# The last iterations of the front, and a new order of the block sums, in a fused attention, mixture-of-experts and softplus kernel

## The chip, the cores and the metric

The kernel runs on one core of a Trainium2 chip. The metric is the time of one execution on the device in microseconds (us); of several executions the median counts. A profile is one further execution, recorded by the hardware profiler. PE is TensorE, PEld its weight loads, DVE VectorE, ACT ScalarE, POOL GpSimd and SP SyncE.

## The reference

Three layers follow each other, in float32.

```
attention:  k, v averaged over blocks of 8 positions (576 -> 72); softmax(q k'/8) v'
            4 batches, 8 heads, 576 positions, 64 channels -> x of 2304 tokens x 512
mixture:    P = exp(x w_gate - max); 8 times: rows /= sum, columns /= sum, P *= 2304/8
            out = sum over 8 experts e of P[:, e] * (relu(x w1[e]) w2[e])     w1 512x1024, w2 1024x512
softplus:   out = softplus(x w_in) w_out                                      512x2048, 2048x512
```

## The kernel before

**Products.** A matrix product in float32 precision is three matmuls on parts: each operand is a rounded high part (`hi`, type fp32r) and a remainder (`lo`), and `three` adds hi*hi, lo*hi and hi*lo in PSUM (names such as `xhi`, `w1lo`, `hhi`, `hlo`). ScalarE rounds, GpSimd or VectorE subtracts for the remainder. All these matmuls stand at line L797.

**Block sums.** The first product of a layer is done with seven products of blocks in place of eight (Strassen's scheme). The input, cut into 2x2 blocks, gives the sums t1 to t4 (`t1 = b12 - b11`, `t3 = b22 - b12`, `t2 = b22 - t1`, `t4 = b21 - t2`), the weights of a unit give S1 to S4, and the products A11, A12, A22, S1, S2, S3, S4 (six matmuls of 128x384 each) are put together by VectorE: `u1 = pb + a` after S1, then after S3 `a = pb + a` (`za` in the rows), `pb = pc + a` and `pd = pd + a` (two rows `p<-p,za`), and at last S4 is added onto `pc` and `u1` onto that.

**Phases.** Work goes in units of 256 columns of the hidden layer, for three groups of 768 tokens: the mixture for group 0, then groups 1 and 2, then softplus for the three. In the two phases of groups 1 and 2 of the mixture (`TWICE`, about 620 to 1560 us) the second product has the block scheme too: two units form a pair, an even and an odd one, and a pair has seven "forms" (`h_slot`, numbered 0 to 6) which are made from the units' results by VectorE, rounded by ScalarE, and multiplied by forms of w2 (`form_product`, twelve matmuls).

**The order of the work** is written out by hand; each engine runs its instructions in program order. The loop `todo` issues `first n+1` before `second n`. `first_twice` issues the products of a unit; `second_twice` of an even unit issues forms 0 and 1, of an odd one forms 2 to 6, and after the first form product of each it calls `go_on`, which issues S4 of the unit whose `first_twice` went before. Between the products lie `posts`: `odd_posts` and `even_posts` multiply the results of a unit by the shares of its expert (`shared`, tile `pb`, L889) and make forms. What `odd_posts` leaves over goes into the list `later`, which the next even unit's `first_twice` works off: `s2` (form 5, ScalarE and GpSimd), `s4` (VectorE difference `d1 - s3`, rounding of form 6), `s1` (VectorE sum into `a21`, named `a` in the rows, form 4) and the remainder of form 6 (VectorE, L896). The shares of an expert, 128 copies of 768 numbers, are loaded by `load_shares` from the last odd unit of the expert before.

**The front** is the start: attention of steps m = 0 to 11 (`front(k)`: scores and softmax of step k, transposes of k - 2, the mixing product `px` of k - 2), whose results are tokens 0 to 767 of x, the input of group 0. In its last iterations (11 to 13, `AHEAD` is 12) it also does the beginning of unit 0 through `fill`. The other attention steps follow inside the first phase: `hook()` runs the next quarter of a step, or an entry of the list `side` (the gate's normalisation: `sk_max`, `sk_max_t`, ...).

Of the kernel before, what the change touches and what calls it, by code (L numbers as in the profile page):

```python
# [19 lines left out]
def attention_moe_softplus_kernel(  # L20
# [223 lines left out]
        pool_sub(lo, raw_form(q), hi.bitcast(F32))  # L244
        load_form(q + 4)

    def load_shares(i):
        if i < len(TWICE) * E:
            m, e = divmod(i, E)
            n = LARGE // P  # L250
            src = pd.rearrange("(t e) p -> e t p", e=E)[e, m * n:(m + 1) * n]
            nc.sync.dma_start(
                pb[0].rearrange("p (t n) -> p t n", n=P), src.partition_broadcast(P)
            )

    def load_w(which, n):
# [249 lines left out]
    def turn_attn():  # L506
# [6 lines left out]
            nc.scalar.copy(aT[:, h, :], pa[:SP, :W])  # L513
        to_mix.append((m, aT))

    def mix():
        m, aT = to_mix.pop(0)
        hb, hp = divmod(m, HP)
        vp = vp_t[kv_of(m)]
        px = bank("px")  # L520
        for h in range(2):
            nc.tensor.matmul(px[h * D:(h + 1) * D, :W], vp[:, h, :], aT[:, h, :])  # L522

        t0 = hb * W
        here = max(0, min(W, TP0 - t0))
        x0 = x_of(0)
        if here < W and hp == 0:
            xb[hb] = at_p.tile([P, KC, W], F32, tag="xb", name="xb")
        if here:
            nc.scalar.activation(x0[:, hp, t0:t0 + here], px[:, :here], AF.Copy, scale=1.0 / POOL)  # L530
        if here < W:
            nc.scalar.activation(xb[hb][:, hp, :], px[:, :W], AF.Copy, scale=1.0 / POOL)
        if here:
            tb = TP0 // 2
            for j in range(2):
                a, z = max(t0, j * tb), min(t0 + here, (j + 1) * tb)
                if a < z and (hp // 2, j) in first_x:
                    hi, lo = (t[:, hp % 2, a - j * tb:z - j * tb] for t in first_x[hp // 2, j])
                    src = px[:, a - t0:z - t0]
                    nc.scalar.activation(hi, src, AF.Copy, scale=1.0 / POOL)  # L540
                    nc.vector.scalar_tensor_tensor(
                        lo, src, 1.0 / POOL, hi.bitcast(F32), op0=ALU.mult, op1=ALU.subtract
                    )
        if hp == HP - 1:
            if here < W:
                nc.sync.dma_start(xd[:, :, max(0, t0 - TP0):t0 + W - TP0], xb[hb][:, :, here:])
            to_gate.append((t0, x0[:, :, t0:t0 + W] if here == W else xb[hb]))
# [25 lines left out]
    def attention():  # L573

        for m in range(AHEAD, STEPS + 2):
            now = [i for i in pooled_at if pooled_at[i] == m]
            while to_gate:
                gate()
            if m + 1 < STEPS:
                channels_first(m + 1)  # L580
            if m < STEPS:
                softmax(m)
            yield
            while to_exp:
                to_exp.pop(0)()
            while to_turn:
                turn_attn()
            for i in pooled_at:
                if pooled_at[i] == m - 1:
                    keys_turned(i)  # L590
            for i in now:
                keys_reduced(i, 0)
            yield
            while to_divide:
                to_divide.pop(0)()
            for i in now:
                values(i)
            yield
            while to_mix:
                mix()  # L600
            for i in now:
                keys_reduced(i, 1)
            yield
# [8 lines left out]
    def front(k, fill=(None, None)):  # L612

        if k < AHEAD:
            softmax(k)
        if to_turn:
            turn_attn()
        if fill[0]:
            fill[0]()
        if k + 1 <= AHEAD:  # L620
            channels_first(k + 1)
        while to_exp:
            to_exp.pop(0)()
        for i in keys_at.get(k, ()):
            keys_summed(i)
        warm((3, 3, 2, 1)[k] if k < 4 else 0)
        while to_divide and (len(to_divide) > 1 or k >= AHEAD):
            to_divide.pop(0)()
        while to_gate:
            gate()  # L630
        if to_mix:
            mix()
        if fill[1]:
            fill[1]()
# [213 lines left out]
    def first_twice(n, between):  # L848

        product = product_of(n)  # L850
        a, u1 = (zpool.tile([P, TB], F32, tag="z", name=x) for x in ("za", "u1"))
        kind = "RL"[sets[n][3] // 2 % 2]
        d1 = two_banks(kind, "p")
        pa, pd_ = d1[:, 0], d1[:, 1]
        product(pa, A11, "b11")
        between(0)
        product(pd_, A22, "t4")
        nc.scalar.copy(a, pa)
        between(1)
        for _ in range(2):  # L860
            if later:
                later.pop(0)()
        d2 = two_banks(kind, "p")
        pc, pb = d2[:, 0], d2[:, 1]
        product(pb, S2, "t2")
        between(2)
        product(pc, S1, "t1")
        vadd(u1, pb, a)
        run_later()
        between(3)  # L870
        product(pa, A12, "b21", True)
        between(4)
        product(pb, S3, "t3", True)
        vadd(a, pb, a)
        vadd(pb, pc, a)
        vadd(pd_, pd_, a)
        between(5)
        two_t[n] = d1, d2

        def s4():  # L880
            product(pc, S4, "b22", True)
            vadd(pc, pc, u1)

        return s4
# [35 lines left out]
    def odd_posts(n):  # L920
# [2 lines left out]
        q = pair_of_units(n) * FORMS  # L923
        d1, d2 = two_t.pop(n)

        def p1():
            shared(d1, d1, 0)
            form_hi(q + 2, d1)

        def p2():  # L930
            shared(d2, d2, 1)
            form_hi(q + 3, d2)
            if u % UPE == UPE - 1:
                load_shares(TWICE.index(f) * E + u // UPE + 1)

        def p3():
            form_lo(q + 2, d1, nc.vector)
# [13 lines left out]
            vsub(d1, d1, s3_t())  # L951
            form_hi(q + 6, d1)

        later.extend([s2, s4, s1, lambda: form_lo(q + 6, d1, nc.vector)])
        return [p1, p2, p3]

    def m_at(f, k):
# [71 lines left out]
                    prep_w2(n + 1)  # L1029
                    load_w(2, n + 2)  # L1030

    def first_parts(n):

        product = product_of(n)
        at = h_tiles(n)
# [21 lines left out]

        def a22():
            product(ps("d"), A22, "t4")

        def s3():
            product(ps("b"), S3, "t3", True)
            add(a, ps("b"), a)
            add(ps("b"), ps("c"), a)
            add(ps("d"), ps("d"), a)

        def a12():
# [22 lines left out]
    def first(n, between, done=None):  # L1090

        do = done or first_parts(n)
        order = ("s2", "a22", "s3") if done else ("m1", "s2", "s1", "a22", "s3", "a12")
        for k, x in enumerate(order):
            do[x]()
            between(k)
# [222 lines left out]
    def finish_attention():  # L1319
# [2 lines left out]
        for i in (2, 3):  # L1322
            g_t[i] = gp.tile([P, GW], F32, name=f"g{i}")
        pools.append(ctx.enter_context(tc.tile_pool(name="tmp", bufs=2)))
        side.extend([to_tiles] + [None] * 6 + [to_prob, None, sk_max, None, sk_max_t, None, None, sk_max_b, None])
        for _ in range(ITERS):
            side.extend([sk_rows, None, None, None, sk_cols])
        side.append(shares_out)
# [68 lines left out]
    def t_lo(eng, name, i, c):  # L1397
# [14 lines left out]
    loads = {  # L1412
# [4 lines left out]
    }  # L1417

    def load(what, i):
# [4 lines left out]
        else:  # L1424
            load_kv(i, k_t if what == "k" else v_t)

    for it in range(AHEAD + 2):
        fill = (None, None)
        if it == AHEAD - 1:
            def fill_in():  # L1430
                xs.update(xs_next)
                unit0.update(first_parts(0))
                unit0["m1"]()
                t_hi("t1", 0, 0)
                t_lo(nc.gpsimd, "t1", 0, 0)
            fill = (fill_in, None)
        if it == AHEAD:
            def fill_in():
# [5 lines left out]
        if it == AHEAD + 1:  # L1444
            def fill_in():
# [1 line left out]
                unit0["s1"]()  # L1447
                t_hi("t2", 1, 0)
                t_lo(nc.vector, "t2", 1, 0)
                t_hi("t4", 3, 0)  # L1450
                t_lo(nc.vector, "t4", 3, 0)
                t_hi("t3", 2, 0)
                t_lo(nc.gpsimd, "t3", 2, 0)
            fill = (fill_in, None)
        front(it, fill)
        if it in (0, 1, 2, 3):
# [10 lines left out]
        for what, i in loads.get(it, ()):  # L1467
            load(what, i)
        if it == 9:
            ectx.close()  # L1470
            hpool = ctx.enter_context(tc.tile_pool(name="h", bufs=1, side="right"))
            zpool = ctx.enter_context(tc.tile_pool(name="z", bufs=2, side="right"))
# [3 lines left out]
            ta, tb = (fpool.tile([P, 2, 2, TP0 // 2], F32, name=x) for x in ("ta", "tb"))  # L1476
            t0_of = lambda i: (ta, tb)[i // 2][:, i % 2]
        if it == 10:
            sums_w1(1)
            parts[1] = w1_parts(1)  # L1480
            x0_sum[1](0)
        if it == 11:
            x0_sum[1](1)
        if it in (12, 13):
            c = it - 12
            x0_sum[2](c)
            x0_sum[4](c)
            x0_sum[3](c)
    t_hi("t2", 1, 1)
    t_lo(nc.vector, "t2", 1, 1)  # L1490
    t_hi("t4", 3, 1)
    t_lo(nc.vector, "t4", 3, 1)
    hook()
    t_hi("t3", 2, 1)
    t_lo(nc.gpsimd, "t3", 2, 1)
    fctx.close()
    h2pool = ctx.enter_context(tc.tile_pool(name="h2", bufs=1, side="right"))
    h_at.append([h2pool.tile([P, UC, LARGE], F32R, name=f"h{x}1") for x in ("hi", "lo")])
# [64 lines left out]
    for step, (what, n) in enumerate(todo):  # L1563
# [3 lines left out]
        if what == "first":  # L1567
# [55 lines left out]
            def between(k):  # L1623
# [2 lines left out]
                    to_split.pop(0)()  # L1626
                if kind == "sp":
                    hook()
                if n or k > 1:
                    hook()  # L1630

            rest = first(n, between, None if n else unit0)
# [14 lines left out]
        else:  # L1647
# [46 lines left out]
                pending.pop(0)()  # L1694
            ahead(f, kind, u)
            if f == 0 and u == NU1 - 6:
                load_shares(0)
            if f == 0 and u == NU1 - 6:
                f64_t.pop()
            if twice(n + 1):  # L1700
# [37 lines left out]
```

## Time and profile before

| | before |
|---|---|
| median of 3 runs | 1955.19 us (1953.75 to 1955.24) |
| profiled execution | 1954.04 us |
| its span, first to last instruction | 1952.3 us |
| TensorE busy | 1928.6 us, 99% |
| weight loads busy | 1794.4 us, 92% |
| VectorE busy | 1471.4 us, 75% |
| ScalarE busy | 973.6 us, 50% |
| GpSimd busy | 1475.1 us, 76% |
| DMA | 306.56 MB, mean 157 GB/s |
| front, with unit 0 | about the first 65 us |
| pairs of units | one every 29.5 us, 32 pairs |

Busy time counts an instruction's whole record. Matmuls are pipelined and their records overlap, so a busy TensorE need not be at its peak; the distance from the start of one matmul to the next tells more. The time outside the span (1.7 us) belongs to the start and the end of the execution.

### The profile page before, as it was taken

To read this page: it belongs to the slowest core of one execution; us is meant where nothing else is said; L and a number is where in the kernel's file an instruction comes from. 1 tells how busy PE (TensorE), PEld (TensorE's weight loads), DVE (VectorE), ACT (ScalarE), POOL (GpSimd) and SP (SyncE) were. 2 spreads that over 40 slices of the span, in tenths; PEclk is the share of its full clock that TensorE was granted. 3 is DMA by queue.
4 is the path that set the end of the run, shared out by engine and by line. 5 is a ranking of instruction groups with operands and counts; after the bars stand their busy time and mean duration, and the time that the engine had idled before them with its cause. 6 is when DMAs were issued, how large, how long until landed. Compare 5 with 4: busy or idle time off the path is not lost.

```text
span 1952.3 us, 30469 instructions
## 1 busy us (share of the span) xinstructions
PE 1928.6 (99%) x10954; PEld 1794.4 (92%) x10954; DVE 1471.4 (75%) x2339; ACT 973.6 (50%) x1773; POOL 1475.1 (76%) x1142
## 2 busy tenths in 40 slices
PE   9899999999999999999999999999999999999999
PEld 7687888989989999999999999999999999999997
DVE  7775576887667888878988889888789776556455
ACT  6545435433334545545445655455554565565542
POOL 6776667787877788778787798887787879675563
PEclk9999999999999999999999999999999999999999
DMA  7343434555547655554555655555545523523311
GB/s 205 116 150 125 145 125 136 178 178 173 183 151 260 208 165 166 168 181 150 163 176 160 219 168 167 161 174 165 181 153 163 192 93 122 191 89 119 133 65 65
DMA packets 213347, 306.56 MB, mean 157 GB/s; under 512 B 33308, under 2 KB 147532, under 8 KB 212940
## 3 DMA queue, kind: packets, MB, share of 16 engines
q1 hardware_dynamic: 203116, 290.85, 46.4%
q10 hardware_dynamic: 10080, 13.77, 1.9%
q8 instruction: 86, 1.41, 0.3%
q14 instruction: 65, 0.53, 0.1%
HBM read 239.30 MB, written 65.27 MB: 156 GB/s over the span
## 4 chain that ended last, share of the span: by engine, by line
PE 90%; DVE 3%; POOL 2%; ACT 2%; DMA 1%; issue 1%; SPq 0%; ACTq 0%; DVEq 0%; POOLq 0%
PE py L797 45%; PE p L797 42%; POOL w1lo L289 1%; PE px L522 1%; PE s L477 1%; DMA vt<-in_v_dram 1%; PE pa L512 1%; DMA pb<-pd 0%; DVE p L1045 0%; POOL w2lo L289 0%; ACT w1hi L320 0%; DMA w2raw<-td 0%; PE pq L464 0%; ACT xhi L693 0%; DVE za L1045 0%
## 5 line engine op out<-in xcount | busy, mean ns | idle before, releaser
L797 PE MATMUL p<-xhi,w1hi 128*128 128x384 f32 x1680 | 572.7, 341 | 5.1 <-DVE p L1045 1.3
L797 PE MATMUL p<-xlo,w1hi 128*128 128x384 f32 x1680 | 563.0, 335 | 0.1
L797 PE MATMUL p<-xhi,w1lo 128*128 128x384 f32 x1680 | 562.9, 335 | 0.0
L289 POOL TENSOR_TENSOR w2lo<-w2raw,w2hi 128x512 fp32r<-128x512 f32 (+1 forms) x235 | 364.0, 1566 | 113.0 <-ACT w2hi L243 100.0
L289 POOL TENSOR_TENSOR w1lo<-w1raw,w1hi 128x512 fp32r<-128x512 f32 x240 | 239.6, 1021 | 227.0 <-ACT w1hi L320 226.9
L797 PEld LDWEIGHTS p<-xhi,w1hi 128*128 128x128 f32 x1680 | 315.6, 188 | 30.1 <-DVE u L845 14.0
L797 PEld LDWEIGHTS p<-xlo,w1hi 128*128 128x128 f32 x1680 | 315.7, 188 | 5.0 <-DVE xlo L1399 0.4
L797 PEld LDWEIGHTS p<-xhi,w1lo 128*128 128x128 f32 x1680 | 315.5, 188 | 0.0
L289 POOL TENSOR_TENSOR w1lo<-sums,w1hi 128x1024 fp32r<-128x1024 f32 x120 | 289.1, 2409 | 1.9 <-ACT w1hi L320 1.9
L797 PE MATMUL py<-w2hi,hhi 128*128 128x512 f32 x672 | 266.4, 396 | 3.3 <-DVE kbd L420 1.3
L797 PE MATMUL py<-w2hi,hlo 128*128 128x512 f32 x672 | 264.0, 393 | 0.0
L797 PE MATMUL py<-w2lo,hhi 128*128 128x512 f32 x672 | 263.6, 392 | 0.0
L797 PE MATMUL py<-hhi,w2hi 128*128 128x384 f32 x716 | 239.4, 334 | 1.1 <-ACT whi L243 1.1
L797 PE MATMUL py<-hlo,w2hi 128*128 128x384 f32 x716 | 239.2, 334 | 0.0
L797 PE MATMUL py<-hhi,w2lo 128*128 128x384 f32 x716 | 239.2, 334 | 0.0
L845 DVE TENSOR_TENSOR g<-py,g 128x768 f32<-128x768 f32 x210 | 199.6, 950 | 50.1 <-PE py L797 50.1
L892 ACT CAST hhi<-p 128x768 fp32r<-128x768 f32 x128 | 102.8, 803 | 211.0 <-DVE p L889 205.7
L797 PEld LDWEIGHTS py<-w2hi,hhi 128*128 128x128 f32 x672 | 126.4, 188 | 32.9 <-issue 3.6
L797 PEld LDWEIGHTS py<-w2hi,hlo 128*128 128x128 f32 x672 | 126.4, 188 | 27.0
L797 PEld LDWEIGHTS py<-w2lo,hhi 128*128 128x128 f32 x672 | 126.5, 188 | 22.5
L797 PEld LDWEIGHTS py<-hhi,w2hi 128*128 128x128 f32 x716 | 134.4, 188 | 1.5 <-ACT whi L243 1.3
L797 PEld LDWEIGHTS py<-hhi,w2lo 128*128 128x128 f32 x716 | 134.4, 188 | 0.0
(163 smaller groups left out, 3540.3 us busy)
## 6 DMA issues: line engine op xcount, KB each, us to landing
w1raw<-in_moe_w_dram SPq DMA_DIRECT2D x96, 512.0 KB
w2raw<-td SPq DMA_DIRECT2D x128, 256.0 KB
sums<-sd SPq DMA_DIRECT2D x62, 512.0 KB
w2raw<-in_moe_w_dram SPq DMA_DIRECT2D x96, 256.0 KB
w2raw<-in_moe_w_dram SPq DMA_DIRECT2D x32, 512.0 KB
sd<-sums SPq DMA_DIRECT2D x32, 512.0 KB
td<-w2raw SPq DMA_DIRECT2D x64, 256.0 KB
xlo<-xlod SPq DMA_DIRECT2D x35, 384.0 KB
```

What stands on the lines that cost most here:

```text
L289: nc.gpsimd.tensor_tensor(o, a, b, op=ALU.subtract)
L477: nc.tensor.matmul(ps[:QP, j * 2 * SP:(j + 1) * 2 * SP], qT[:, j * QP:(j + 1) * QP], kb)
L512: nc.tensor.transpose(pa[:SP, j * QP:(j + 1) * QP], ex[:, 2 * j + h, :], ident[:QP, :QP])
L522: nc.tensor.matmul(px[h * D:(h + 1) * D, :W], vp[:, h, :], aT[:, h, :])
L797: nc.tensor.matmul(ps, lhs[a], rhs[b], start=first and i == 0, stop=last and i == 2, skip_group_check=goes_on,)
L845: vadd = lambda o, x, y: nc.vector.tensor_tensor(o, x, y, op=ALU.add)
L892: nc.scalar.copy(h_slot(q)[0], src)
```

## The change

What it does, part by part:

- `front`: the `fill` of an iteration is issued after the exponentials, no longer ahead of them.
- Iterations 11 to 13: w1 of unit 1 is loaded after iteration 7 and summed after 9 (before: 8 and 10); the second half of t2 is computed in two parts, the far one from `px` in PSUM; t3 is summed and rounded ahead of t4; S2 of unit 0 is issued right after the front loop, ahead of t4 and the gate; then `first` of unit 0 has S3 and A22 left.
- `first_twice`: the entries of `later` are worked off one, two and one at a time (before: two and two), in the order s2, s1, s4, remainder, and the last one stands between the two sums after S3.
- `load_shares` loads half of the shares at a time, the first half one `post` earlier.
- One more empty entry in `side` between `sk_max` and `sk_max_t`.

```diff
-    def load_shares(i):
+    def load_shares(i, j):
...
+            n = TB // P
+            t = m * 2 * n + j * n
+            src = pd.rearrange("(t e) p -> e t p", e=E)[e, t:t + n]
...
+        if m in on_mix:
+            on_mix[m](px)
         if here:
             tb = TP0 // 2
...
-            if m + 1 < STEPS:
+            if AHEAD < m + 1 < STEPS and m > AHEAD:
                 channels_first(m + 1)
...
         if to_turn:
             turn_attn()
-        if fill[0]:
-            fill[0]()
         if k + 1 <= AHEAD:
             channels_first(k + 1)
         while to_exp:
             to_exp.pop(0)()
+        if fill[0]:
+            fill[0]()
...
         between(1)
-        for _ in range(2):
-            if later:
-                later.pop(0)()
+        if later:
+            later.pop(0)()
         d2 = two_banks(kind, "p")
         pc, pb = d2[:, 0], d2[:, 1]
         product(pb, S2, "t2")
         between(2)
         product(pc, S1, "t1")
         vadd(u1, pb, a)
-        run_later()
+        for _ in range(2):
+            if later:
+                later.pop(0)()
         between(3)
         product(pa, A12, "b21", True)
         between(4)
         product(pb, S3, "t3", True)
         vadd(a, pb, a)
+        run_later()
         vadd(pb, pc, a)
         vadd(pd_, pd_, a)
...
+        def next_shares(j):
+            if u % UPE == UPE - 1:
+                load_shares(TWICE.index(f) * E + u // UPE + 1, j)
+
         def p1():
             shared(d1, d1, 0)
             form_hi(q + 2, d1)
+            next_shares(0)
 
         def p2():
             shared(d2, d2, 1)
             form_hi(q + 3, d2)
-            if u % UPE == UPE - 1:
-                load_shares(TWICE.index(f) * E + u // UPE + 1)
+            next_shares(1)
...
-        later.extend([s2, s4, s1, lambda: form_lo(q + 6, d1, nc.vector)])
+        later.extend([s2, s1, s4, lambda: form_lo(q + 6, d1, nc.vector)])
...
-    def first_parts(n):
+    def first_parts(n, done_first=False):
...
         def a22():
             product(ps("d"), A22, "t4")
+            if done_first:
+                onto_d()
 
         def s3():
             product(ps("b"), S3, "t3", True)
             add(a, ps("b"), a)
             add(ps("b"), ps("c"), a)
+            if "d" in got:
+                onto_d()
+
+        def onto_d():
             add(ps("d"), ps("d"), a)
...
-        order = ("s2", "a22", "s3") if done else ("m1", "s2", "s1", "a22", "s3", "a12")
+        order = ("s3", "a22") if done else ("m1", "s2", "s1", "a22", "s3", "a12")
...
-[to_prob, None, sk_max, None, sk_max_t, None, None, sk_max_b, None])
+[to_prob, None, sk_max, None, None, sk_max_t, None, None, sk_max_b, None])
...
+    far = 2 * W - TP0 // 2
+
+    def near_t2(px):
+        nc.vector.tensor_tensor(
+            t0_of(1)[:, 1, :far], on_b(1, 1)(1)[:, :far], t0_of(0)[:, 1, :far], op=ALU.subtract
+        )
+
+    def far_t2(px):
+        nc.vector.scalar_tensor_tensor(
+            t0_of(1)[:, 1, far:], px[:, :TP0 - 2 * W], 1.0 / POOL, t0_of(0)[:, 1, far:],
+            op0=ALU.mult, op1=ALU.subtract,
+        )
+        t_hi("t2", 1, 1)
+        t_lo(nc.vector, "t2", 1, 1)
+        x0_sum[3](1)
+        t_hi("t3", 2, 0)
+        t_lo(nc.gpsimd, "t3", 2, 0)
+
+    on_mix.update({AHEAD - 2: near_t2, AHEAD - 1: far_t2})
...
         if it == 11:
             x0_sum[1](1)
-        if it in (12, 13):
-            c = it - 12
-            x0_sum[2](c)
-            x0_sum[4](c)
-            x0_sum[3](c)
-    t_hi("t2", 1, 1)
-    t_lo(nc.vector, "t2", 1, 1)
-    t_hi("t4", 3, 1)
-    t_lo(nc.vector, "t4", 3, 1)
+            t_lo(nc.gpsimd, "t1", 0, 0)
+        if it == 12:
+            x0_sum[2](0)
+            x0_sum[3](0)
+            next(parts[1])
+        if it == 13:
+            t_hi("t3", 2, 1)
+            t_lo(nc.gpsimd, "t3", 2, 1)
+    channels_first(AHEAD + 1)
+    xs["t2"] = xs_next["t2"]
+    unit0["s2"]()
+    for c in range(2):
+        x0_sum[4](c)
+        t_hi("t4", 3, c)
+        t_lo(nc.vector, "t4", 3, c)
+    while to_gate:
+        gate()
     hook()
-    t_hi("t3", 2, 1)
-    t_lo(nc.gpsimd, "t3", 2, 1)
...
-                if n or k > 1:
+                if n or k in (0, 6):
                     hook()
```

## Rows read from the trace of the kernel before

**Rows 1.** Windows: stretch, busy time of each engine, granted TensorE clock, DMA.
```profile
80.00:83.30 3.30, 3.30 (x9) 2.73 (x10) 1.44 (x2) 3.15 (x8) 1.73 (x2) 0.50 0.94 276
...
640.00:1560.00 920.00, 917.42 (x5217) 902.42 (x5215) 791.14 (x1069) 478.29 (x761) 742.50 (x516) 1.00 0.54 172
```

**Rows 2.** Waits of TensorE, whole span: us in total, times, longest.
```profile
PE pg L555 <- ACT xb L532: 1.7, 1, 1.7
...
PE py L797 <- DVE kbd L420: 1.3, 1, 1.3
PE p L797 <- DVE p L1045: 1.3, 1, 1.3
...
PE py L797 <- ACT whi L243: 1.1, 1, 1.1
...
PE pm L1184 <- DVE big L1180: 0.9, 1, 0.9
```

**Rows 3.** Waits of the weight loads, 640 to 1560 us.
```profile
PEld p L797 <- DVE u L845: 14.0, 48, 0.6
```

**Rows 4.** Timeline of VectorE, even unit: start, duration, instruction, idle before.
```profile
1149.16 0.97 DVE L846 TENSOR_TENSOR p<-p,s 128x768 f32<-128x768 f32 x1
1150.04 0.55 DVE L845 TENSOR_TENSOR u<-p,za 128x384 f32<-128x384 f32 x1
1150.50 0.95 DVE L845 TENSOR_TENSOR a<-p,a 128x768 f32<-128x768 f32 x1
1151.37 0.95 DVE L896 TENSOR_TENSOR hlo<-p,hhi 128x768 fp32r<-128x768 f32 x1
1152.23 0.55 DVE L845 TENSOR_TENSOR za<-p,za 128x384 f32<-128x384 f32 x1
1152.82 1.03 DVE L845 TENSOR_TENSOR p<-p,za 128x384 f32<-128x384 f32 x2
```

**Rows 5.** Timeline of ScalarE, the same even unit.
```profile
1150.17 0.80 ACT L892 CAST hhi<-p 128x768 fp32r<-128x768 f32 x1 [0.17 <-DVE p L846]
```

**Rows 6.** Timeline of TensorE, the same even unit: A12, S3, form 2, S4.
```profile
1149.43 0.33 PE L797 MATMUL p<-xhi,w1hi 128*128 128x384 f32 x1
...
1150.64 0.45 PE L797 MATMUL p<-xhi,w1hi 128*128 128x384 f32 x1
...
1151.80 0.33 PE L797 MATMUL py<-hhi,whi 128*128 128x384 f32 x1
...
1153.88 0.33 PE L797 MATMUL p<-xhi,w1hi 128*128 128x384 f32 x1
```

**Rows 7.** Timeline of VectorE, the odd unit before it.
```profile
1138.22 0.56 DVE L845 TENSOR_TENSOR u<-p,za 128x384 f32<-128x384 f32 x1 [0.89 <-PE p L797]
...
1140.27 0.56 DVE L845 TENSOR_TENSOR za<-p,za 128x384 f32<-128x384 f32 x1 [0.16 <-PE p L797]
```

**Rows 8.** Timeline of TensorE, the odd unit: first matmuls of A12 and form 0.
```profile
1137.95 0.33 PE L797 MATMUL p<-xhi,w1hi 128*128 128x384 f32 x1
...
1140.07 0.33 PE L797 MATMUL py<-hhi,w2hi 128*128 128x384 f32 x1
```

**Rows 9.** Instructions on tile `a`: durations in ns, first and last start.
```profile
L845 DVE TENSOR_TENSOR a<-p,a x32: 946/947/949, 646.2 to 1565.0; 128x768 f32<-128x768 f32 x32
```

**Rows 10.** Timeline of VectorE in the front.
```profile
50.47 0.61 DVE L497 TENSOR_REDUCE s<-s 96x6 f32<-96x432 f32 x1 [1.61 <-ACT s L492]
...
53.55 1.23 DVE L1390 TENSOR_TENSOR ta<-g,ta 128x384 f32<-128x384 f32 x1
...
64.13 1.03 DVE L1045 TENSOR_TENSOR p<-p,za 128x384 f32<-128x384 f32 x2
```

**Rows 11.** Windows, VectorE alone: busy time, granted clock, DMA.
```profile
65.00:80.00 15.00, 14.57 (x31) 1.00 0.41 122
```

**Rows 12.** Timeline of GpSimd in the front.
```profile
53.35 1.01 POOL L1390 TENSOR_TENSOR tb<-g 128x384 f32<-128x384 f32 x1
```

More of the change, by code (lines that the diff above doesn't have):

```diff
@@ L245, in prep_form @@
         load_form(q + 4)
-    def load_shares(i):
+    def load_shares(i, j):
         if i < len(TWICE) * E:
             m, e = divmod(i, E)
-            n = LARGE // P
-            src = pd.rearrange("(t e) p -> e t p", e=E)[e, m * n:(m + 1) * n]
+            n = TB // P
+            t = m * 2 * n + j * n
+            src = pd.rearrange("(t e) p -> e t p", e=E)[e, t:t + n]
             nc.sync.dma_start(
-                pb[0].rearrange("p (t n) -> p t n", n=P), src.partition_broadcast(P)
+                pb[0][:, j * TB:(j + 1) * TB].rearrange("p (t n) -> p t n", n=P), src.partition_broadcast(P)
             )
@@ L514, in turn_attn @@
         to_mix.append((m, aT))
+    on_mix = {}
     def mix():
@@ L1324, in finish_attention @@
         pools.append(ctx.enter_context(tc.tile_pool(name="tmp", bufs=2)))
-        side.extend([to_tiles] + [None] * 6 + [to_prob, None, sk_max, None, sk_max_t, None, None, sk_max_b, None])
+        side.extend([to_tiles] + [None] * 6 + [to_prob, None, sk_max, None, None, sk_max_t, None, None, sk_max_b, None])
         for _ in range(ITERS):
@@ L1431, in fill_in @@
                 xs.update(xs_next)
-                unit0.update(first_parts(0))
+                unit0.update(first_parts(0, True))
                 unit0["m1"]()
                 t_hi("t1", 0, 0)
-                t_lo(nc.gpsimd, "t1", 0, 0)
             fill = (fill_in, None)
@@ L1449, in fill_in @@
                 t_lo(nc.vector, "t2", 1, 0)
[L1450 to L1453, printed above, removed]
             fill = (fill_in, None)
@@ L1469, in attention_moe_softplus_kernel @@
         if it == 9:
+            sums_w1(1)
+            parts[1] = w1_parts(1)
             ectx.close()
@@ L1478, in attention_moe_softplus_kernel @@
         if it == 10:
-            sums_w1(1)
-            parts[1] = w1_parts(1)
             x0_sum[1](0)
@@ L1696, in attention_moe_softplus_kernel @@
             if f == 0 and u == NU1 - 6:
-                load_shares(0)
+                load_shares(0, 0)
+                load_shares(0, 1)
             if f == 0 and u == NU1 - 6:
```

4 rows, old and new, of the table loads are left out of this document.

## The prediction

> **What bounds the kernel now.** I read the page first. TensorE is busy for 1928.6 of the 1952.3 us of the span, so a change can only move the time through the places where TensorE stands still or runs slowly. These I looked for in three views. The windows [rows 1] show TensorE at half its clock, 1.2 GHz, in one stretch only, 80.0 to 83.3 us, and the two phases with shared block sums (640 to 1560 us) with TensorE at 917.4 of 920. The list of what TensorE waited for [rows 2] holds only single stops of 0.9 to 1.7 us, nearly all before 80 us. But a matmul's record is 0.33 us long while the next begins 0.17 us after it, so a short stop leaves no idle time in TensorE's row. The weight loads [rows 3] show it: in 640 to 1560 they stood 14.0 us behind the vector sum `u`, 48 times. So there are two places to work out: the front up to 80 us, which happens once, and a stop that returns with every pair of units. A small cost there counts 31 times.
>
> **The order of the block sums in `first_twice` (the largest term).** I take one even unit, the one at 1149 us, and count from T = 1149.43, when its product A12 begins [rows 6]; a product of six matmuls takes 1.04 (0.174 each).
>
> Before, VectorE does the S4 difference (`p<-p,s`) ahead of `u`, so `u` ends at 1150.59 and S3, which overwrites what `u` reads, begins at 1150.64 and not at T + 1.04 = 1150.47 [rows 4, 6]. The restart costs too: S3's six matmuls last from 1150.64 to 1151.80, 1.16 and not 1.04. Loss: 0.17 + 0.12 = 0.29 us. The next gate is S4 of the same unit: it adds onto the tile that the sum `pb + a` reads, so it waits for that sum. Product S3 (1.04) and form product 2 (twelve matmuls, 2.08) lie between, S4 begins at 1153.88, and the sum, the first of the two `p<-p,za`, ended at 1152.82 + 0.56 = 1153.38, a sum of that size taking 0.56 [rows 4, 6, 7]: 0.50 to spare.
>
> After, VectorE's order is `u`, S1 sum, S4 difference, `za`, remainder of form 6, `pb + a`. Step by step:
> - `u` no longer has anything ahead of it. In the odd unit, which has none of these extras, it starts 0.27 after A12 begins (1138.22 against 1137.95) [rows 7, 8]: T + 0.27, done at T + 0.83. S3 starts on time at T + 1.04; the 0.29 is gone.
> - S1 sum at T + 0.73 (0.46 after `u`, rows 4). S4 difference 0.87 later, T + 1.60, and 0.97 long: done T + 2.57.
> - `za` needs S3: in the odd unit it starts 0.20 after the next product begins [rows 7, 8], here T + 2.28, but VectorE is free at T + 2.48.
> - The remainder of form 6 needs ScalarE's rounding of the S4 difference: 0.04 after it, 0.80 long [rows 5], done T + 3.41. So VectorE starts the remainder at T + 3.45 and `pb + a` 0.86 later, T + 4.31; done T + 4.87.
> - S4 could begin at T + 1.04 + 1.04 + 2.08 = T + 4.16. It now begins 0.04 after the sum, T + 4.91, and pays the restart: 0.75 + 0.12 = 0.87 us lost.
>
> The remainder, which waits on ScalarE, has been put ahead of the sum on which TensorE waits, and behind it VectorE stands still. Net: 0.87 - 0.29 = +0.58 us for each even unit that has such leftovers. Their number is that of the S1 sums, 32, less the last one, at 1565.0, which lies after the phases [rows 9]: 31. **31 x 0.58 = +18.0 us.** Bounds: -0.29 a unit (S4 keeps its cover: -9.0 us) and +0.87 (the old stop stays as well: +27); I take +0.58, since every step has its own row.
>
> **The front.** Rounding t1 now stands behind the exponential, not ahead of it. VectorE's row sum for step 11 waited 1.61 us, until 50.47, for that exponential [rows 10] and can start when step 10's division ends, at 48.9. From there I add up, with the durations of the same operations in the same stretch: division 1.7 (50.6), transposes 1.3, ScalarE's copies 1.8 (they stand behind the rounding of w1 that is put ahead of them), mixing product 0.6: 54.3. The second half of t2 then comes straight from the product in PSUM: 0.3 to start, remainder of the first half 0.55, sum 0.4, rounding 0.5, remainder 0.56, last matmuls of S2 0.6: S2 ends at 57.2, and the gate's stop of 1.7 us [rows 2] lies under it. Yet unit 0's S4 needs a VectorE sum that stands in its queue behind all of t4: `u` 0.55, t4's two sums and two remainders with two waits for a rounding 3.2, softmax of step 12 1.2, `za` and the sum 1.15. That is 63.3; before, it ended at 64.13 + 0.56 = 64.7 [rows 10]. From 65 to 80 us VectorE is busy for 14.57 of 15 us [rows 11], so what follows only shifts: the stop behind `kbd` [rows 2] and the slow stretch remain. **-1.4 us.** Bounds: -4.4, the stops of TensorE between 46 and 65 us (the largest, 1.7 and 1.3, in rows 2); and +1.7, if the 1.9 us in which TensorE now waits ahead of S4 pull the clock to 1.2 GHz once more, half of the 3.4 us that this took at 80 us [rows 1]. Loading and summing w1 of unit 1 an iteration earlier fills an idle GpSimd (four sums, 2.9 us); without that cover t1's sum, and with it all of the front, would come up to 2.9 later.
>
> The t2 sum of the first half took 1.23 us at 53.55, a sum of the same size 0.56, while GpSimd worked from 53.35 to 54.36 [rows 10, 12]. The Trainium skill, SBUF — State Buffer, section "Who interferes with whom", says why: VectorE with two SBUF inputs and GpSimd take one port pair in turn, each for a whole instruction. The trace agrees: 54.36 plus most of 0.56 is 54.78, where that sum ended. By that rule one t4 sum, now beside GpSimd's t3 remainders, loses 0.6 more, and the front gains 0.8, not 1.4.
>
> **The smaller edits.** One more empty slot ahead of `sk_max_t`: the stop of 0.9 us on `big` [rows 2] and its restart go: -1.0 (bounds 0 and -1.0). The shares come in two halves, the first one a step earlier: the stop of 1.1 us on `whi` [rows 2] sits behind a VectorE product that had to wait for `pb`; **-1.1** (bounds 0, and -1.1). SyncE issues 16 more transfers; each waits for a VectorE product ahead of the one that SyncE waits for already, so nothing is queued longer: 0. The number of `hook()` calls in unit 0 stays two: 0.
>
> **Sum** against the profiled execution, whose time was 1954.04 (span 1952.3): 1954.04 + 18.0 - 1.4 - 1.0 - 1.1 = 1968.5. The median of the three runs is 1.15 above that execution, so the forecast for a median is 1969.7, 0.74% slower.
>
> **Rivals.**
> 1. *S4 keeps its cover* (faster). The 0.50 us to spare and a faster rounding suffice, and only the old stop goes: 1955.2 - 9.0 - 3.5 = 1942.7. For it: the stop ahead of S3 is plain in the rows. Against: the sum is behind the remainder in one queue, and the chain S4 difference, rounding, remainder is 0.97 + 0.80 + 0.86 long after T + 1.60. It decides from the point where the remainder starts before T + 2.7. Chance 0.11.
> 2. *The rounding is early, the order alone costs.* If the remainder started right behind `za` (T + 2.94), `pb + a` would end at T + 4.36, S4 be 0.24 + 0.12 late, and the units lose 0.07 each, 2.2 us: 1955.2 + 2.2 - 3.5 = 1953.9, no change. Against: the rounding cannot start before T + 2.57. Chance 0.06.
> 3. *The form product takes the tile that the remainder still reads.* Form product 2 would then wait from T + 2.08 to T + 4.35: 31 x 2.1 = 65 us, 2017. Against: in the trace that product began at 1151.80 (T + 2.37) while the remainder ran until 1152.32 [rows 4, 6], so its tile is another. Chance 0.03.
>
> **How the numbers follow.** Forecast 0.80, of which 1963 to 1976 holds nearly all (front -4.4 to +1.7, the units 16 to 20 us). About 0.2%, 3.9 us, can be told from no change. Faster 0.12 (rival 1), same 0.06 (rival 2), slower 0.82. The range of 8 in 10 reaches a little below the forecast's own for units that lose half of what I count: 1958 to 1976.
>
> **What would show it.** Right: in even units VectorE's order `u`, `a`, `p<-p,s`, `za`, `hlo`, `p<-p,za`, with `hlo` waiting for ScalarE; S4's first matmul 0.7 to 0.9 us late behind that sum; S3 without a stop; the period of a pair longer by 0.6 us; 9 us more in each of the two phases; S4 of unit 0 about 1.4 us earlier. Wrong: the weight loads' wait on `u` gone and nothing in its place, and the phases shorter by 4.5 us each.

## The result, and the profile after

| | before | after |
|---|---|---|
| median of the timed runs, us | 1955.22 (1953.75 to 1955.90) | 1969.68 (1969.12 to 1974.73) |
| ratio, 95% interval | 1 | 1.0081 [1.0063, 1.0098] |
| span of the profiled execution, us | 1952.3 | 1968.1 |
| its time, us | 1954.04 | 1969.96 |

The changed kernel is 0.8% slower; the forecast was 1969.7. That the two medians agree to 0.1 us is luck: the forecast for the profiled execution, to which the sum was made, was 1968.5, and it took 1969.96. The line numbers of `first_twice` and of what stands behind it have moved by a few: L797 is now L802, L845 is L850, L1045 is L1056, L896 is L903.

The first view is TensorE's waits over the whole span (us in total, times, longest). Three of the five single stops of [rows 2] are gone (`pg`, `py` on `whi`, `pm`). What is new stands on top: 31 stops behind a `p` that VectorE writes. The stop behind L1056 is that ahead of unit 0's S4, 1.3 before.

```profile
PE p L802 <- DVE p L850: 17.6, 31, 0.6
...
PE p L802 <- DVE p L1056: 1.6, 1, 1.6
PE py L802 <- DVE kbd L421: 1.3, 1, 1.3
```

The same list for the weight loads, 640 to 1560 us, answers to [rows 3]: the wait on `u` has fallen from 14.0 us (48 times) to 5.0 (22 times), and 27.5 us behind the same 31 sums have come. So 26 stops on `u` went, where the forecast had counted 31.

```profile
PEld p L802 <- DVE p L850: 27.5, 31, 1.0
PEld p L802 <- DVE u L850: 5.0, 22, 0.3
```

The even unit that answers to [rows 4], VectorE (start, duration, instruction, and in brackets the idle time before it and what ended it). `u` now comes ahead of `a` and of the S4 difference `p<-p,s`; then VectorE stands still for 0.41 us behind ScalarE's rounding, and the sum that S4 needs is the first of the two at 1161.68, of 0.56 us each.

```profile
1157.64 0.56 DVE L850 TENSOR_TENSOR u<-p,za 128x384 f32<-128x384 f32 x1 [0.56 <-PE p L802]
1158.12 0.95 DVE L850 TENSOR_TENSOR a<-p,a 128x768 f32<-128x768 f32 x1
1158.98 0.96 DVE L851 TENSOR_TENSOR p<-p,s 128x768 f32<-128x768 f32 x1
1159.84 0.55 DVE L850 TENSOR_TENSOR za<-p,za 128x384 f32<-128x384 f32 x1
1160.80 0.96 DVE L903 TENSOR_TENSOR hlo<-p,hhi 128x768 fp32r<-128x768 f32 x1 [0.41 <-ACT hhi L899]
1161.68 1.02 DVE L850 TENSOR_TENSOR p<-p,za 128x384 f32<-128x384 f32 x2
```

TensorE in the same unit, answering to [rows 6]: the first matmul of A12, the first of S3, the last of form product 2, and the first two of S4.

```profile
1157.37 0.33 PE L802 MATMUL p<-xhi,w1hi 128*128 128x384 f32 x1
...
1158.42 0.34 PE L802 MATMUL p<-xhi,w1hi 128*128 128x384 f32 x1
...
1161.39 0.34 PE L802 MATMUL py<-hhi,wlo 128*128 128x384 f32 x1
1162.29 0.44 PE L802 MATMUL p<-xhi,w1hi 128*128 128x384 f32 x1 [0.56 <-DVE p L850]
1162.57 0.34 PE L802 MATMUL p<-xlo,w1hi 128*128 128x384 f32 x1
```

S3 begins 1.05 after A12, with no stop. S4 begins 0.90 after the matmul ahead of it, where 0.174 is the distance of two matmuls that run on: 0.73 late. The distance to the next is 0.28, another 0.11: 0.84 in all.

Where the time went can be read by laying the two traces side by side, matmul by matmul, since both hold the same 10954 matmuls in the same order but for the front (worked out from the starts of single matmuls, so no row of a view). From 45 to 84 us the changed kernel loses 0.2 us; at `sk_max` (245 us) it gains 1.04; at 329 us 0.49; from 630 to 1570 us it loses 17.1; behind 1570 nothing. With 0.2 lost in the first 45 us and small steps between, the last matmul comes 16.0 later; the spans differ by 15.8.

The 17.1 us are made up like this. S4's new stop costs 0.84 on average in each of the 31 even units that have leftovers, 26.0 us. S3's old stop of 0.28 is gone in 26 of them, 7.2 us; of the other five, three (near 645, 1090 and 1120 us) had no stop ahead of S3 before, and two (near 795 and 1061) keep theirs. Near 1098 us 1.2 us are gained, and a few single stops elsewhere give some 0.6 more.

### The profile page after: what moved, and what is told of

The parts are those of the page before. It is cut to its first block, busy times and chain, and to the rows that moved or that the text cites. A ratio compares the mean times of both kernels' runs of the same rounds, so it can differ in the third digit from the quotient of the medians.

```text
span 1968.1 us, 30492 instructions
## 1 busy us (share of the span) xinstructions
PE 1932.5 (98%) x10954; PEld 1797.2 (91%) x10954; DVE 1470.7 (75%) x2340; ACT 973.0 (49%) x1773; POOL 1475.8 (75%) x1142
## 4 chain that ended last, share of the span: by engine, by line
PE 87%; DVE 8%; issue 2%; ACT 2%; POOL 1%; ACTq 0%; DVEq 0%; POOLq 0%
PE py L802 43%; PE p L802 40%; DVE p L851 2%; ACT hhi L899 1%; DVE hlo L903 1%; DVE p L850 1%; PE s L478 1%; DVE u L850 1%; PE px L525 1%; PE pa L513 1%; PE pk L433 0%; PE warm L615 0%; PE pq L465 0%; ACT w1hi L321 0%; DVE p L1056 0%
## 5 line engine op out<-in xcount | busy, mean ns | idle before, releaser
L802 PE MATMUL p<-xhi,w1hi 128*128 128x384 f32 x1680 | 574.8, 342 | 22.0 <-DVE p L850 17.6
L802 PE MATMUL p<-xlo,w1hi 128*128 128x384 f32 x1680 | 564.6, 336 | 0.9 <-DVE xlo L1416 0.5
L802 PE MATMUL p<-xhi,w1lo 128*128 128x384 f32 x1680 | 564.2, 336 | 0.0
L802 PEld LDWEIGHTS p<-xhi,w1hi 128*128 128x128 f32 x1680 | 316.4, 188 | 48.4 <-DVE p L850 27.8
L802 PEld LDWEIGHTS p<-xlo,w1hi 128*128 128x128 f32 x1680 | 316.6, 188 | 6.6 <-DVE xlo L1416 2.0
L802 PEld LDWEIGHTS p<-xhi,w1lo 128*128 128x128 f32 x1680 | 316.4, 188 | 0.0
L802 PE MATMUL py<-w2hi,hhi 128*128 128x512 f32 x672 | 266.4, 396 | 2.6 <-DVE kbd L421 1.3
L802 PE MATMUL py<-w2hi,hlo 128*128 128x512 f32 x672 | 264.0, 393 | 0.0
L802 PE MATMUL py<-w2lo,hhi 128*128 128x512 f32 x672 | 263.6, 392 | 0.0
L802 PE MATMUL py<-hhi,w2hi 128*128 128x384 f32 x716 | 239.3, 334 | 0.0
L802 PE MATMUL py<-hhi,w2lo 128*128 128x384 f32 x716 | 239.3, 334 | 0.0
L802 PE MATMUL py<-hlo,w2hi 128*128 128x384 f32 x716 | 239.2, 334 | 0.0
L850 DVE TENSOR_TENSOR g<-py,g 128x768 f32<-128x768 f32 x210 | 199.8, 952 | 50.2 <-PE py L802 50.2
L802 PEld LDWEIGHTS py<-w2hi,hhi 128*128 128x128 f32 x672 | 126.5, 188 | 32.2 <-issue 3.6
L802 PEld LDWEIGHTS py<-w2hi,hlo 128*128 128x128 f32 x672 | 126.4, 188 | 27.1
L903 POOL TENSOR_TENSOR hlo<-s,hhi 128x768 fp32r<-128x768 f32 x64 | 118.7, 1854 | 37.8 <-ACT hhi L899 36.4
L802 PEld LDWEIGHTS py<-w2lo,hhi 128*128 128x128 f32 x672 | 126.5, 188 | 22.4
L802 PEld LDWEIGHTS py<-hhi,w2lo 128*128 128x128 f32 x716 | 134.4, 188 | 0.0
```

The source lines that it names most:

```text
L802: nc.tensor.matmul(ps, lhs[a], rhs[b], start=first and i == 0, stop=last and i == 2, skip_group_check=goes_on,)
L850: vadd = lambda o, x, y: nc.vector.tensor_tensor(o, x, y, op=ALU.add)
L903: eng.tensor_tensor(lo, src, hi.bitcast(F32), op=ALU.subtract)
```

## The experiments

Each ratio is to the kernel before, run on the same chip.

**e1: the changed kernel with the old order of the block sums.**

```
         between(1)
-        if later:
-            later.pop(0)()
+        for _ in range(2):
+            if later:
+                later.pop(0)()
...
         vadd(u1, pb, a)
-        for _ in range(2):
-            if later:
-                later.pop(0)()
+        run_later()
...
         vadd(a, pb, a)
-        run_later()
...
-        later.extend([s2, s1, s4, lambda: form_lo(q + 6, d1, nc.vector)])
+        later.extend([s2, s4, s1, lambda: form_lo(q + 6, d1, nc.vector)])
```

> The changed kernel with only first_twice's working-off of the leftovers put back (order s2, s4, s1, remainder; two and two). Theory (the remainder ahead of the sum pb + a makes S4 wait in 31 units): all of the 18 us of the units go, and what is left of the change is the front, the empty slot and the half shares: 1969.7 - 18 = 1951.7. Rival (the front or the shares carry part of the slowdown): it stays above 1955.

Measured: 1952.69, ratio 0.9986 [0.9976, 0.9997]. Without the new order the change is a small gain. The new stops are gone, and the old ones on `u` are back (weight loads, 620 to 1600 us):

```profile
PEld p L802 <- DVE u L850: 14.3, 49, 0.6
```

**e2: the kernel before with the new order alone** (the same lines the other way round).

> The kernel before with only first_twice's new order. Theory: 31 units x 0.58 us = +18: 1955.2 + 18 = 1973.2, slower than the whole change, with TensorE waiting for the sum p (L845 or near it) 31 times and no stop on u. Rival (the slowdown needs the front or the shares as well): under 1970.

Measured: 1973.10, ratio 1.0090 [1.0076, 1.0105]. The order alone makes all of the loss: by the traces 18.6 us from 630 to 1570 us, with the gains at 245 and 329 us absent. TensorE's waits, whole span:

```profile
PE p L797 <- DVE p L845: 17.9, 31, 0.6
```

**e3: the changed kernel with the remainder of form 6 behind both sums.**

```
         vadd(a, pb, a)
-        run_later()
         vadd(pb, pc, a)
         vadd(pd_, pd_, a)
+        run_later()
```

> The changed kernel with one line moved: the remainder of form 6 is issued behind the two sums after S3, not between them. Theory: the sum pb + a then ends near T + 3.6, before S4 wants to begin (T + 4.16), and u is on time as well, so both stops go: 1969.7 - 31 x 0.87 = 1942.7. Rival (VectorE has too much to do there, and a later wait takes the place: form product 4 on the sum of form 2, up to 0.15 + 0.12 a unit): up to 1951.

Measured: 1954.19, ratio 0.9986 [0.9973, 0.9999]. The loss is gone, so it was the remainder's place ahead of the sum. But the 1942.7 did not come, and its trace says why. VectorE in an even unit: the remainder follows the two sums without any idle time, the S4 stop is gone, and yet VectorE works without a break until 1158.8, so that the onto-sum of form product 4 (`g<-py,g`, 1157.83) ends at 1158.77.

```profile
1150.38 1.03 DVE L850 TENSOR_TENSOR p<-p,za 128x384 f32<-128x384 f32 x2
1151.32 0.95 DVE L903 TENSOR_TENSOR hlo<-p,hhi 128x768 fp32r<-128x768 f32 x1
...
1156.97 0.95 DVE L903 TENSOR_TENSOR hlo<-p,hhi 128x768 fp32r<-128x768 f32 x1
1157.83 0.94 DVE L850 TENSOR_TENSOR g<-py,g 128x768 f32<-128x768 f32 x1
```

Form product 6 takes that sum's tile. TensorE's row shows no idle time, but the distances are 0.25 and 0.26 and not 0.174:

```profile
1158.67 0.34 PE L802 MATMUL py<-hhi,w2lo 128*128 128x384 f32 x1
1158.92 0.41 PE L802 MATMUL py<-hhi,w2hi 128*128 128x384 f32 x1
1159.18 0.34 PE L802 MATMUL py<-hlo,w2hi 128*128 128x384 f32 x1
```

Over 640 to 1560 us the weight loads count 28 such stops (the profile puts them down to `issue`; that the sum is behind them is what e5 tests):

```profile
PEld py L802 <- issue: 5.5, 28, 0.2
```

So 26 stops of S3 with 7.2 us became 28 in the form products with 5.5 us, and some single ones: the 0.87 us of VectorE's time was handed on to a later product, not saved. The expectation's rival had named that kind of wait, at another product (4) and with a lower time (1951).

**e4: the changed kernel, with the S4 difference ahead of the S1 sum.**

```
-        later.extend([s2, s1, s4, lambda: form_lo(q + 6, d1, nc.vector)])
+        later.extend([s2, s4, s1, lambda: form_lo(q + 6, d1, nc.vector)])
```

> The changed kernel with the S4 difference ahead of the S1 sum in the list of leftovers (s2, s4, s1, remainder), positions as changed. ScalarE's rounding of form 6 is then done near T + 2.6, when za ends, so VectorE doesn't stand still for it; the remainder is still ahead of pb + a. Theory (the loss has two parts, the wait for the rounding and the remainder's own 0.86 in the queue): S4 is 0.24 + 0.12 late, not 0.75 + 0.12: 1969.7 - 31 x 0.5 = 1954. Rival (the queue place alone does it): it stays near 1969; rival (the wait alone does it): S4 is on time, 1943.

Measured: 1963.59, ratio 1.0033 [1.0020, 1.0046]; above the theory's 1954 and below the rival's 1969. With the difference first, VectorE no longer stands still for the rounding (the remainder starts right behind `za`). But form product 2 now stops behind the S1 sum `a`, the later of the two. It is not the sum's value that it needs: ScalarE began to round that at 1156.41 only. The product begins 0.05 after the sum's end; by the program it takes a pair of PSUM banks that held block sums of the pair of units before, which that sum reads. VectorE, ScalarE and TensorE of e4:

```profile
1154.56 0.96 DVE L851 TENSOR_TENSOR p<-p,s 128x768 f32<-128x768 f32 x1
1155.43 0.95 DVE L850 TENSOR_TENSOR a<-p,a 128x768 f32<-128x768 f32 x1
1156.29 0.55 DVE L850 TENSOR_TENSOR za<-p,za 128x384 f32<-128x384 f32 x1
1156.76 0.94 DVE L903 TENSOR_TENSOR hlo<-p,hhi 128x768 fp32r<-128x768 f32 x1
1157.62 1.02 DVE L850 TENSOR_TENSOR p<-p,za 128x384 f32<-128x384 f32 x2
```

```profile
1156.41 0.84 ACT L899 CAST hhi<-a 128x768 fp32r<-128x768 f32 x1
```

```profile
1153.82 0.33 PE L802 MATMUL p<-xhi,w1hi 128*128 128x384 f32 x1
...
1156.43 0.44 PE L802 MATMUL py<-hhi,whi 128*128 128x384 f32 x1 [0.34 <-DVE a L850]
...
1158.62 0.33 PE L802 MATMUL p<-xhi,w1hi 128*128 128x384 f32 x1
```

The stop is 0.51 + 0.11 = 0.62 in each even unit. In 26 of them before lost 0.28 at S3, in the other five nothing is saved: 26 x 0.34 + 5 x 0.63 = 12.0 us, and single stops elsewhere give 0.8 back; the two traces differ by 11.2 from 630 to 1570 us. The expectation had looked at the remainder alone and not at the tile that the S1 sum holds.

S4 has no stop here, but that is no sign against the theory. The sum that it needs ended at 1157.62 + 0.56 = 1158.18, 4.36 after A12 (1153.82), which is late by the 0.24 that was expected; S4 began at 1158.62 only because form product 2 had pushed it back. So e4 does not show what the wait for the rounding costs S4 by itself.

**e5: e3 with the remainder of form 0 one product later.** If VectorE's backlog is all that is late in e3, moving one 0.95 us instruction that nobody needs yet should do.

```
             if posts:
                 posts.pop(0)()
             elif pending:
                 pending.pop(0)()
-            if k == 3 and posts:
-                posts.pop(0)()
```

> The kernel of e3 (remainder of form 6 behind both sums), and the remainder of form 0 taken one product later, behind the onto-sum of form 4 instead of right behind the rounding of S3. In e3 the stop ahead of S4 was gone, but in each even unit form product 6 stood 0.08 + 0.08 us (and form product 4 mostly 0.04 more) behind the onto-sum of form 4 (g<-py,g), which stood behind the remainders in VectorE's queue. Theory (VectorE's queue is the only thing late there, by 0.87 us for the one moved remainder): that stop goes, 31 x 0.16 to 0.19 = 5 to 6 us less than e3, ratio to before about 0.9957, some 1947.4 for a before of 1955.8. Rival A (something else than VectorE's queue holds form product 6, its tile or its weights): same as e3, 1953. Rival B (the late remainder of form 0 holds a product of the next odd unit): a new stop there, 1953 or more.

Measured: 1948.40, ratio 0.9961 [0.9946, 0.9976], faster than both kernels and near the theory's 1947.4. The onto-sum now stands ahead of that remainder, and form product 6 waits for nothing. VectorE, an even unit:

```profile
1154.75 0.96 DVE L850 TENSOR_TENSOR g<-py,g 128x768 f32<-128x768 f32 x1
1155.62 0.95 DVE L903 TENSOR_TENSOR hlo<-p,hhi 128x768 fp32r<-128x768 f32 x1
1156.83 0.96 DVE L850 TENSOR_TENSOR g<-py,g 128x768 f32<-128x768 f32 x1 [0.26 <-PE py L802]
```

The gain over e3 between 630 and 1570 us is 4.9 us by the traces, of which 28 units make 4.2, 0.15 each.

**e6: e5 with `u` ahead of a piece of the float64 conversion**, behind which it stands in odd units.

```
         product(pb, S2, "t2")
+        vadd(u1, pb, a)
         between(2)
         product(pc, S1, "t1")
-        vadd(u1, pb, a)
```

> The kernel of e5, and the sum u of first_twice issued right behind product S2, ahead of the hook in which VectorE gets a piece of the float64 conversion. In odd units u stands 0.3 us behind such a piece, and S3 pays 0.06 + 0.11 us for it in each (before, after and e3 alike). Theory (a stop of TensorE that returns in each of 31 odd units is worth its length times 31, whoever makes it): 5.2 us less than e5, some 1942.2 for a before of 1955.8. Rival A (u ahead only makes VectorE stand still for 0.3 us, and the next sum za or the product with the shares comes late by as much): same as e5, 1947. Rival B (the conversion falls behind its due times): a stop of several us once, 1945 or more.

Measured: 2013.56, ratio 1.0294 [1.0279, 1.0310], a wide miss. S1 now waits for `u` in every unit, not in odd ones alone. By the program the two share one thing: products S2 and S1 write the two halves of one tile, and the sum, issued ahead of S1, reads that tile. TensorE's waits, 640 to 1630 us, and one of the 62:

```profile
PE p L802 <- DVE u L850: 55.6, 62, 1.1
```

```profile
1149.24 0.34 PE L802 MATMUL p<-xhi,w1lo 128*128 128x384 f32 x1
1150.30 0.44 PE L802 MATMUL p<-xhi,w1hi 128*128 128x384 f32 x1 [0.72 <-DVE u L850]
```

**e7: e5 with `u` behind S1 as there, and still ahead of the conversion.**

```
         product(pb, S2, "t2")
-        between(2)
         product(pc, S1, "t1")
         vadd(u1, pb, a)
+        between(2)
```

> The kernel of e5, with u issued behind product S1 as there, but ahead of the hook with the piece of the float64 conversion (e6 had u ahead of product S1, and S1 then waited 0.88 + 0.10 us for it in every unit, since both products of a pair lie in one tile: TensorE's stop on u was 62 x 0.98 = 61 us). Theory: with the order of S1 and u as before, S1 waits for nothing, and in odd units u begins when S1 ends and no longer 0.3 us later; S3's stop of 0.06 + 0.11 us goes, 31 x 0.17 = 5.2 us less than e5, some 1943.2 for a before of 1955.5. Rival A (za or a later sum is late by as much, since VectorE stands still ahead of u): same as e5, 1948.4. Rival B (e6 lost by the order of u and the conversion's piece, and not by that of u and S1): some 2013 again.

Measured: 1958.85, ratio 1.0018 [1.0007, 1.0029], 10 us more than e5. Rival B is out, so it was the order of `u` and S1 that cost in e6; rival A was right in kind and too small. The stop on `u` is gone, but the piece had filled a hole. With `u` ahead of it VectorE stands still for 1.21 us, four pieces then come in a row, and the sum ahead of S4 is late:

```profile
1168.84 0.56 DVE L850 TENSOR_TENSOR u<-p,za 128x384 f32<-128x384 f32 x1 [1.21 <-PE p L802]
...
1171.48 0.69 DVE L1293 TENSOR_TENSOR dt<-da,dt 128x512 f32<-128x512 f32 x1
1172.09 0.55 DVE L850 TENSOR_TENSOR za<-p,za 128x384 f32<-128x384 f32 x1
1172.67 1.03 DVE L850 TENSOR_TENSOR p<-p,za 128x384 f32<-128x384 f32 x2
```

```profile
1172.56 0.34 PE L802 MATMUL py<-hhi,wlo 128*128 128x384 f32 x1
1173.29 0.44 PE L802 MATMUL p<-xhi,w1hi 128*128 128x384 f32 x1 [0.39 <-DVE p L850]
```

The weight loads (640 to 1560 us) count 22 of them:

```profile
PEld p L802 <- DVE p L850: 14.8, 22, 0.7
```

22 x (0.56 + 0.11) is 14.7. Against them stand the stops on `u` that went: 22 in e5, by the weight loads, and not the 31 of the expectation; most were 0.17 long, 3.7 us for all. With single stops that went as well the traces of e7 and e5 differ by 9.5 us from 630 to 1570 us. It is the fault of the change once more, in odd units: an instruction that has to wait stands in VectorE's queue ahead of the sum that S4 needs.

## Why the prediction was right, and where a term was not

**The order of the block sums: right, step by step.** Counted from A12 (1157.37 here), forecast against measured: `u` 0.27 and 0.27; S1 sum 0.73 and 0.75; S4 difference 1.60 and 1.61; `za` 2.48 and 2.47; remainder 3.45 and 3.43; the sum 4.31 and 4.31; S4 4.91 and 4.92. S3 lost its stop. The mechanism is the one forecast. That the phases then fit to 0.2 us (17.1 measured, 18.0 - 1.1 forecast) is in part luck. S4's stop came to 26.0 us where 31 x 0.87 = 27.0 was forecast, but S3's gave back 7.2 and not 31 x 0.29 = 9.0: the prediction took all 31 units to have had that stop, and only 26 lost one. The order by itself is thus 18.9 us (18.6 in the traces of e2), and single stops elsewhere hid the difference. e2 shows that the order alone makes the loss, e1 that nothing else does, and e3 that the remainder's place is the part of the order that costs.

**Rival 1 was out, but its price was wrong too.** It had put 1942.7 on the case that S4 keeps its cover. e3 makes that case by moving the remainder, at 1954.19. The rival let the old stop go and looked for nothing behind it; what was late next was form product 6, on the same queue of VectorE.

**Rival 2** had the sum end 4.36 after A12 if the rounding is early, and in e4 it did; but the S1 sum, moved behind the difference, stopped form product 2, so its price for the units was too low. **Rival 3** was out for the remainder, beside which form product 2 ran on; its mechanism (a product that takes a tile still being read) is what e4 met with the other sum, and e6 with `u`.

**The front: mis-sized.** Forecast -1.4 to unit 0's S4 and from there on; measured in the profiled execution, reckoned from 45 us, -0.7 at S4 and +0.2 at 84 us. Two things were off. First, the sum ahead of S4 ended at 64.19 and not 63.3. Two VectorE instructions put at 0.55 took about twice that: the remainder of the first half of t2 took 0.97, its twin at 56.38 0.56, and `u` started at 57.64, 0.4 later than the 57.2 on which it was to follow; the first t4 sum took 1.11, its twin at 60.29 0.55. VectorE, then GpSimd, of the changed kernel:

```profile
54.56 0.97 DVE L1416 TENSOR_TENSOR xlo<-ta,xhi 128x384 fp32r<-128x384 f32 x1 [0.58 <-ACT xhi L1412]
...
56.38 0.56 DVE L1416 TENSOR_TENSOR xlo<-ta,xhi 128x384 fp32r<-128x384 f32 x1 [0.58 <-ACT xhi L1412]
...
57.64 0.56 DVE L1056 TENSOR_TENSOR u<-p,za 128x384 f32<-128x384 f32 x1 [0.26 <-PE p L802]
58.11 1.11 DVE L1407 TENSOR_TENSOR tb<-g,ta 128x384 f32<-128x384 f32 x1
...
60.29 0.55 DVE L1407 TENSOR_TENSOR tb<-g,ta 128x384 f32<-128x384 f32 x1
...
63.62 0.57 DVE L1056 TENSOR_TENSOR p<-p,za 128x384 f32<-128x384 f32 x1
```

```profile
53.52 1.59 POOL L290 TENSOR_TENSOR w1lo<-w1raw,w1hi 128x512 fp32r<-128x512 f32 x1
...
56.84 1.97 POOL L1416 TENSOR_TENSOR xlo<-tb,xhi 128x384 fp32r<-128x384 f32 x2 [0.44 <-ACT xhi L1412]
```

Each ran beside a GpSimd instruction and ended 0.4 us after it: GpSimd was done at 55.11 and 58.81, VectorE at 55.53 and 59.22. The Trainium skill, SBUF — State Buffer, section "Who interferes with whom", has a VectorE instruction with two SBUF inputs and a GpSimd instruction that reads SBUF take turns at one port pair. The trace agrees, and the gain of 0.8 us by that rule was nearer than the 1.4 that the forecast took; the prediction had applied that rule to the t4 sum alone. In the traces of e1 and e3 to e7, which share the changed front, S4 of unit 0 came 0.6 to 0.7 us earlier than before too, and by 90 us 0.7 to 0.8 were still there.

Second, the upper bound's case did occur in this one execution: the granted clock was 1.2 GHz for 6.8 us, from within the 1.60 us wait ahead of S4, twice the 3.4 us by which that bound was priced. The window of the changed kernel (stretch, busy times of the five engines, granted clock, DMA), and the same in e3:

```profile
63.27:70.10 6.83, 5.86 (x18) 5.84 (x19) 6.69 (x14) 3.72 (x8) 6.46 (x6) 0.50 0.32 95
```

```profile
63.27:70.10 6.83, 5.96 (x39) 5.65 (x39) 6.69 (x14) 3.89 (x8) 6.60 (x5) 1.00 0.31 91
```

Against e3 it cost 2.6 us by 70 us and only 0.9 to 1.0 by 84: VectorE was busy for 6.69 of these 6.83 us in both, so TensorE, slow or fast, soon stood behind it again.

**The small edits.** The extra empty slot: -1.04, forecast -1.0. The gain of 0.49 at 329 us, where a stop of 0.54 behind ScalarE's `g<-py` is gone, was not foreseen; e1 and e3 to e7 have it, e2 has not; which edit brings it was not taken apart. The shares: -1.2, forecast -1.1, but not for the reason given. In e1 `pb` came in time and yet the same unit stopped for 1.20 us, now behind the transfer of `xlo`, which SyncE issues between the two halves of the shares (1090.87) and for which a matmul of S4 stood still until 1099.35. The prediction had put the order of the transfers at 0, since nothing would be queued longer; that step did not hold. In the changed kernel S4 is 0.72 us late in that unit anyway, and `xlo` (issued at 1094.30) was there when its first matmul asked for it at 1102.36. So with the old order the split only passed the stop to the next transfer; how much of the 1.2 us is the cover of S4's stop and how much an earlier landing was not taken apart.

**Against the sum:** 1968.5 was forecast for the profiled execution, which took 1969.96: the front was 1.6 worse, the two phases 0.2 and the first 45 us 0.2, and 329 us was 0.5 better.

## What to carry to other kernels

An instruction that must wait for another engine (here a remainder behind a rounding) goes behind every sum that TensorE is waiting for, not ahead of one; what it costs is its own length plus the wait, less what the sum had to spare, in every round (here about 0.86 + 0.41 - 0.50 us, and 0.11 for the restart), and that outweighed all the other edits together. When a stop is seen in one round, count the rounds that have it: here 26 of 31. When a stop is taken away, add up the queue of the engine behind it to the end of the round: e3 gained 1.6 us where 13 were expected, until e5 moved the one instruction with time to spare. Before a read is moved ahead of a product, see which tile that product writes: in e6, with two halves of one tile, the product waited in every unit, and the kernel was 65 us slower than e5.

## What the runs showed of the hardware

- A stop costs more than its wait. After these stops of S1, S3 and S4 the first two matmuls stood 0.28 us apart and not 0.174, whether the wait was 0.17 us (`u`, before) or 0.9 (e6): about 0.11 us on top each time. In the form products of e3 it was 0.08.
- The same front, with nearly the same wait of 1.5 to 1.6 us ahead of unit 0's S4, got its low clock at different places. In the changed kernel's profile the clock fell within that wait (63.3 to 70.1 us at 1.2 GHz). In e1, e3 and e7 it stayed at 2.4 GHz through it. In e4, e5 and e6 it had been at 1.2 GHz for 3.4 us before and was at 2.4 GHz again by the time of the wait; in e5 TensorE had stood still for at most 0.52 us at a time in the 10 us ahead of that. e2, with the front of before, shows such a stretch too, from 59.0 us. Neither the edit nor the length of the pause settles it; what does, these runs leave open. The row is of e5:

```profile
56.89:60.30 3.41, 3.32 (x39) 2.38 (x39) 2.09 (x5) 1.57 (x5) 1.96 (x2) 0.50 0.36 87
```

- A low stretch need not cost. In e5 S4 of unit 0 still came 0.66 us earlier than before, in e3, without that stretch, 0.64: S4 waits for a VectorE sum, and TensorE was early.
